# Moving chunk 1's logit transposes and maximum in the first gate/up, and building an edge constant with three GpSimd instructions

## The chip, the cores and the metric

The kernel runs on one core of a Trainium2 chip. A core has a matrix engine (TensorE, "PE" in the profile, its weight loads "PEld"), a vector engine (VectorE, "DVE"), an activation engine (ScalarE, "ACT"), a general engine (GpSimd, "POOL") and a queue engine that issues transfers (SyncE, "SP"). Each engine runs its own instruction stream in order and meets the others through semaphores. The metric is the device time of one execution in microseconds; of several executions the median counts.

## What is computed

One transformer block with modulation (adaLN). `x` is 2048 rows of 576 in bfloat16, `c` one row of 576. The two branches are an attention in which every row sees 8 earlier rows, two apart, and a gated feed-forward without a nonlinearity of width 4608. Cut to what matters:

```python
mod = (_silu(c) @ w_mod).reshape(c.shape[0], 6, 1, -1)
sa, ca, ga, sb, cb, gb = ...
h = _layernorm(x) * (1 + ca) + sa
x = x + ga * A(h)          # 32 heads of 18; idx = pos - 2 * arange(8), masked below 0
h = _layernorm(x) * (1 + cb) + sb
x = x + gb * (((h @ w_gate) * (h @ w_up)) @ w_down)
# A: logits = einsum('bhsd,bhswd->bhsw', q, k[idx]) / sqrt(18)
#    o = einsum('bhsw,bhswd->bhsd', softmax(logits), v[idx]);  o @ wo
```

## The kernel before

The 2048 rows are cut into 8 chunks of 256. A prologue (to about 48.7 us) computes the modulation and takes chunk 0 through its norm, its queries, keys and values and its attention. Then the chunks go through the feed-forward in the groups [0], [1, 2], [3, 4], [5, 6], [7]; for each group `gate_up` (L907) runs 36 row-tile pairs and `down` (L950) the product with `w_down`. A pair (`wg_pair`, L745) computes 128 columns of gate and of up: the contraction of 576 is four blocks of 128 rows and a rest of 64, and each matmul works on 64 rows, so that two of them share the PE array, one for `pg` (gate) and one for `pu` (up), each in a PSUM bank of its own. `first()` of a pair starts with the rest rows, whose weights lie in `wgr`, then takes the weights of its block (`wgu`, or `hh` for a block that was loaded there ahead of time); `second()` follows behind the next pair's `first()`. ACT copies `pu` (L796) and `pg` (L797) to SBUF, and in the first group DVE multiplies two pairs at a time into `hh` (L799).

Everything that the later chunks need before their turn runs between these pairs: in the first gate/up the attention of chunks 1 and 2, the norm of chunk 3 and its queries, keys and values, the norm of chunk 4, and the last part of the modulation. This work is cut into pieces, tuples of (PE time, DVE time, marks needed, mark set, delay of that mark, call). They are listed in threads, and a planner (`timed`, L847) sets them between the pairs with a simple clock of PE and DVE; in each step it takes the first thread whose next piece is ready. The order in which the calls are made is the order of the instructions on every engine; nothing is reordered afterwards.

The names that the change touches, with the lines of the kernel before:

- Chunk attention. `prod_t` (L485): products of q with the shifted k, one window position per instruction on DVE, eight per chunk. `b_l` (L494): PE sums them over the head dimension into `lgT`, four positions at a time; ACT copies `lgT` to `lgs` (L497). For chunk 1, `b_lt` (L505) has PE transpose `lgs` into a PSUM tile `lg`, four transposes; for the other chunks a transfer does it (L511, into `lg_t`). `b_sm0`: DVE takes the maximum `mx` over the eight positions (L521) and subtracts it into `dd` (L522). `b_exp` (L514): ACT's exponential of `dd`. Then `ssum` (L694), its reciprocal by ACT (L695, L697) and the shares `attn` (L702), the products with the shifted values `vsh` (L542) and their sums (L549 to L552) into `o_sb`. All PSUM tiles come from one pool of 8 banks: a bank that `lg` holds is free for a pair when `dd` has been written.
- Values. `v_sb` is stored to DRAM (`vd`, L470) and loaded back shifted (`vsh`, L479), both by POOL.
- Norm of a chunk: statistics on DVE (L281 to L285), ACT's roots and factors (L288 to L293), ACT's `xn` (L306), for chunk 3 in four pieces; a transposing transfer of `xn` into `hT` by SP (L418) and the modulation on DVE (L321).
- The last part of the modulation, `gb` (`gb_row` L1301, `gb_cols`): PE multiplies `sc_bc` with the last 576 columns of `w_mod` into `pa` (L378); ACT copies it (L381), and POOL stores it to DRAM (L382) and loads it back to all partitions (L383). The columns of `w_mod` are loaded by `load_wm5`: POOL clears a rest tile (L1055) and issues the load of 576 KB into a part of `hh` that is not in use yet (L1056) and of 72 KB into the rest tile, an `o_t` buffer (L1057). Right behind it POOL issues the first load of `w_down` (L174).
- Edge constant. In the prologue, chunk 0's second half of 128 rows takes shares of the first half's last rows through two constants, `edge` (L247 to L250) and `edge_t` (L252 to L256; 128 x 16 with ones at 2 + 18w + n for the seven positions w, n below 14 - 2w). PE reads `edge_t` in L608. `share_j` (L1139) makes chunk 0's shares on DVE (L1140), and `shift_attn` (L568) reads them on PE into `pz`.

Of the kernel before, what the change touches and what calls it, by code (L numbers as in the profile page):

```python
# [7 lines left out]
BF = mybir.dt.bfloat16  # L8
F32 = mybir.dt.float32
ALU = mybir.AluOpType  # L10
ACTF = mybir.ActivationFunctionType
AX = mybir.AxisListType
# [6 lines left out]
P = 128  # L19
# [6 lines left out]
W = 8  # L26
DIL = 2
FF = 4608
FT = FF // P
HALO = 16  # L30
SPAN = 14
# [14 lines left out]
def kernel(  # L46
# [13 lines left out]
    nc = tc.nc  # L60
# [31 lines left out]
    def ps(shape, dt, name):  # L92
        return psp.tile(shape, dt, name=name, tag="bank")

    def js(j):
        return slice(j * P, (j + 1) * P)
# [25 lines left out]
    def product(n):  # L122
        k0 = (prod_n[0] % (4 * CH // n)) * KT * n
        prod_n[0] += 1
        return prod_t[:, k0:k0 + KT * n].rearrange("p (k n) -> p k n", k=KT)

    sp_guard = tc.tile_pool(name="setup", bufs=1)
    sp = sp_guard.__enter__()
# [4 lines left out]
    def x_rows(i):  # L133
        return x_flat[i * CH:(i + 1) * CH, :].rearrange("(j p) d -> p j d", p=P)

    def load_x(i):
        if i < NCH:
            x_in[i] = xin.tile([P, ST, D], BF, name="x_t")
            nc.sync.dma_start(x_in[i][:], x_rows(i))
# [73 lines left out]
    for xn_t in xns:  # L213
# [12 lines left out]
                            pattern=[[-1, P + 2 * SPAN]], channel_multiplier=1)  # L226
# [4 lines left out]
    for k in range(2):  # L231
# [5 lines left out]
                            pattern=[[P, KT], [-DH, H]], channel_multiplier=1)  # L237
    nc.gpsimd.affine_select(out=ind[:], in_=ind[:], compare_op=ALU.is_ge, fill=0.0, base=DH - 1,
                            pattern=[[-P, KT], [DH, H]], channel_multiplier=-1)
    nc.gpsimd.memset(maskneg[:], 0.0)  # L240
    nc.gpsimd.affine_select(out=maskneg[:], in_=maskneg[:], compare_op=ALU.is_ge, fill=NEG,
                            base=-DIL * (W - 1), pattern=[[DIL, W], [0, H]], channel_multiplier=1)
    edge = sp.tile([P, W - 1, P], BF, name="edge")
    edge_t = sp.tile([P, 2 * HALO], BF, name="edge_t")[:, 0:HALO]
# [4 lines left out]
                            pattern=[[-(HALO + DIL), W - 1], [1, P]], channel_multiplier=-1)  # L249
    nc.gpsimd.affine_select(out=edge[0:HALO], in_=edge[0:HALO], compare_op=ALU.is_ge, fill=0.0, base=SPAN - 1,  # L250
                            pattern=[[-DIL, W - 1], [0, P]], channel_multiplier=-1)
    nc.gpsimd.memset(edge_t[:], 0.0)  # L252
    for w in range(W - 1):
        d = edge_t[:, 0:SPAN - DIL * w]
        nc.gpsimd.affine_select(out=d, in_=d, compare_op=ALU.not_equal, fill=1.0, base=-DIL - (HALO + DIL) * w,
                                pattern=[[-1, SPAN - DIL * w]], channel_multiplier=1)  # L256
    nc.gpsimd.memset(wo[64:, KF, :], 0.0)
    nc.gpsimd.memset(oT[64:, KF, :], 0.0)
    nc.gpsimd.memset(o_sb[:, :, D:], 0.0)
# [150 lines left out]
    def a_t(i, on_dve=True):  # L410
        a_tiles(i)
        hT = aa[i]["hT"]
        transposed(aa[i]["xn"], lambda m: hT[:, m, :], (0, 1), 0)(on_dve)
# [6 lines left out]
    def a_t4():  # L420
        a_t(4, False)
        nc.gpsimd.memset(aa[4]["hT"][64:, KF, :], 0.0)
# [27 lines left out]
    def a_q(i, g):  # L450
        qk_tiles(i, QGRP[g], slice(0, CH), nc.scalar.copy)
        if g == 2:
            a_halo(i)
# [34 lines left out]
    def b_l(i, w0):  # L488
        b = bb[i]
        prods = [b["prod"].pop(w0 + c) for c in range(4)]  # L490
        lgT = ps([P, CH], F32, "lgT")
        for m in range(KT):
            for c in range(4):
                nc.tensor.matmul(lgT[H * c:H * (c + 1), :], lhsT=ind[:, m, :], rhs=prods[c][:, m, :],  # L494
                                 start=(m == 0), stop=(m == KT - 1), skip_group_check=True)
        lgs = lgsp.tile([P, CH], BF, name="lgs")
        nc.scalar.copy(lgs[:], lgT[:])  # L497
        b.setdefault("lgs", []).append(lgs)

    def b_lt(i):  # L500
        b = bb[i]
        b["lg"] = ps([P, ST, W, H], BF, "lg")
        for w0, lgs in zip((0, 4), b.pop("lgs")):
            for j in range(ST):
                nc.tensor.transpose(b["lg"][:, j, w0:w0 + 4, :].rearrange("p w h -> p (w h)"), lgs[:, js(j)], ident[:])  # L505
# [7 lines left out]
    def b_exp(i):  # L513
        nc.scalar.activation(bb[i]["dd"][:], bb[i]["dd"][:], ACTF.Exp, scale=scale)  # L514
# [118 lines left out]
    def b_od(i):  # L633
        for j in range(ST):
            nc.sync.dma_start_transpose(out=oT[:, :, js(j)], in_=o_sb[:, j, :])
# [45 lines left out]
    def prods_of(i):  # L681
        r = []
        for w in (0, 4):
            r += [(0, 0.82, "", f"p{i}{v}", 1.0, lambda v=v: b_p(i, v)) for v in range(w, w + 4)]
            r += [(0.75, 0, f"p{i}{w + 3}", f"l{i}{w}", 1.0, lambda w=w: b_l(i, w)), (0, 0, f"l{i}{w}", f"t{i}{w}", 9.0 if i == 7 else 6.0, lambda w=w: b_ltd(i, w))]
        return r

    def softmax_of(i):
        b1 = lambda: b_sm1(i)
        if i in GROUPS[1]:  # L690
            def total():
                b = bb[i]
                ssum = small.tile([P, ST, H], F32, name="ssum")
                nc.vector.tensor_reduce(ssum[:], b["dd"][:].rearrange("p j w h -> p j h w"), axis=AX.X, op=ALU.add)  # L694
                nc.scalar.activation(ssum[:], ssum[:], ACTF.Ln)  # L695
                b["rs"] = small.tile([P, ST, H], F32, name="rs")
                nc.scalar.activation(b["rs"][:], ssum[:], ACTF.Exp, scale=-1.0)  # L697

            def shares():
                b = bb[i]  # L700
                b["attn"] = attnp.tile([P, ST, W, H], BF, name="attn")
                nc.vector.tensor_tensor(b["attn"][:], b.pop("dd")[:], b.pop("rs")[:, :, None, :].to_broadcast([P, ST, W, H]), ALU.mult)  # L702
            return [(0, 1.4, f"t{i}4", "y1", 0.0, lambda: b_sm0(i, False)) if i == 1 else (0, 1.4, f"t{i}4", f"s{i}", 1.1, lambda: b_sm0(i)), (0, 1.05, f"s{i}", f"r{i}", 0.9, total), (0, 0.72, f"r{i}", f"a{i}", 0.0, shares)]
        return [(0, 1.4, f"t{i}4", f"s{i}", 1.1, lambda: b_sm0(i)), (0, 2.4, f"s{i}", f"a{i}", 0.0, b1)]

    def values_of(i, nxt=None):
        r = []
        for j in range(ST):
            r += [(0, 0.75, f"a{i}", "-", 0, lambda j=j, w=w: b_mul(i, j, w)) for w in range(0, W, 2)]
            r += [(0, 0.75, "", "-", 0, lambda j=j: b_add(i, j, 0)), (0, 0.75, "", "-", 0, lambda j=j: b_add(i, j, 1)),  # L710
                  (0, 1.2, "", f"o{i}{j}", 0, lambda j=j: b_add(i, j, 2))]
            if nxt is not None:
                r.append((0, 0, f"v{nxt}", "-", 0, lambda j=j: b_ld(nxt, j)))
        return r

    def attention_of(c1, c2):
        p2, sm = prods_of(c2), softmax_of(c1)
        first = prods_of(c1) + p2[:4] + sm[:1] + p2[4:6] + sm[1:] + p2[6:]
        return first + values_of(c1, c2) + [(0, 0, "", "-", 0, lambda: b_od(c1))] + softmax_of(c2) + values_of(c2)
# [334 lines left out]
    def load_wm5():  # L1054
        nc.gpsimd.memset(wm5r[64:, :], 0.0)  # L1055
        nc.gpsimd.dma_start(wm5(), w_mod[0:KF * P, 5 * D:6 * D].rearrange("(k p) n -> p k n", p=P))  # L1056
        nc.gpsimd.dma_start(wm5r[0:64, :], w_mod[KF * P:D, 5 * D:6 * D])  # L1057
# [49 lines left out]
    def pj(j, w):  # L1107
        off = HALO - DIL * (W - 1 - w) + j * P
        prods[j, w] = product(P)
        nc.vector.tensor_tensor(prods[j, w], aa[0]["qT"][:, :, js(j)], aa[0]["kT"][:, :, off:off + P], ALU.mult)  # L1110
# [28 lines left out]
    def share_j(j):  # L1139
        nc.vector.tensor_tensor(attn0[:, j], dd0[:, j], sums.pop(j)[:, None, :].to_broadcast([P, W, H]), ALU.mult)  # L1140
# [50 lines left out]
        lj(1, w)  # L1191
    pj(1, 4)
    pj(1, 5)
    share_j(0)
    a_q(1, 1)
    shift_attn(0)
# [104 lines left out]
    def gb_row():  # L1301
# [2 lines left out]

    first = attention_of(1, 2)[12:-14]
    first = [(0, 0, "", "p17", 2.2, nop), (0.75, 0, "p17", "l14", 1.0, lambda: b_l(1, 4)), (0.35, 0, "l14", "t14", 0.3, lambda: b_lt(1))] + first
    second = attention_of(3, 4)
    second[1] = (*second[1][0:2], "n2", *second[1][3:])
    at = [k for k, p in enumerate(first) if p[2] == "v2"][0]
# [3 lines left out]
    first[at] = (0.6, 0, "o11", "-", 0, lambda: b_o(1))  # L1313
    gbg = {0: (qkv_of(3, "p17 z3"),
               [[(0, 0, "", "-", 0, lambda: (load_wm5(), load_wd(0))), (0, 0, "", "z3", 8.0, both_halves), (0, 0, "", "w5", 12.0, nop), (0.85, 0, "w5", "-", 0, gb_row), (0, 0, "", "-", 0, lambda: load_res(2))],
                first, [(0, 0, "y1", "s1", 0.6, lambda: b_exp(1))],
                norm_of(3, "", "", 5) + [(0, 2.5, "", "m4", 0.2, lambda: a_ln(4)), (0, 0, "m4", "r4", 1.0, lambda: aa[4]["rsq"]()),
                                         (0, 0, "r4", "e4", 2.0, lambda: aa[4]["norm"]((0,))), (0, 0, "e4", "n4", 1.6, lambda: aa[4]["norm"]((1,))),
                                         (0.6, 0, "n4 v3", "x4", 0, lambda: (a_t4(), load_x(6)))]]),
           1: (qkv_of(5, "p37"),  # L1320
               [[(0, 0, "", "-", 0, lambda: (loads_v(3), load_res(3), load_res(4)))], norm_of(5, "p33", "", 7), second]),
           2: (qkv_of(6, ""),
# [33 lines left out]
    for gi, grp in enumerate(GROUPS):  # L1356
        hh_t = hhp.tile([P, FT * 2 * CH], BF, name="hh")
        n = CH * len(grp)
# [45 lines left out]
```

## Time and profile before

| | before |
|---|---|
| median of 3 runs | 544.89 us (544.35 to 546.2) |
| profiled execution | 545.29 us |
| span of its profile | 543.6 us |
| mean granted TensorE clock | 1.000 |
| PE busy | 534.2 us (98%) |
| DVE busy | 316.4 us (58%) |
| ACT busy | 252.4 us (46%) |
| POOL busy | 71.1 us (13%) |

All times of the trace are microseconds from the span's start. A row of the timeline gives the start, the busy time, the engine, the line, the operation, what it writes and reads, the shape, and in square brackets the idle time of the engine before it with what ended that wait. Consecutive instructions of one kind are drawn together in one row with their count. A row that ends in "POOLq" or "PEldq" tells of an engine's queue: the semaphores that it went through ahead of an instruction. The line "DMA to landing" gives the time from a transfer's issue to its last byte's arrival, smallest, median and largest.

### The profile page before, as it was taken

The numbers are of one execution on the slowest core, as the hardware profiler recorded it, in microseconds if no ns is written. First come the engines' busy times: TensorE is split into PE (matmuls) and PEld (weight loads), VectorE is DVE, ScalarE is ACT, GpSimd is POOL, SyncE is SP. The second block draws the span as 40 slices with busy tenths as digits, with TensorE's granted clock in tenths as the row PEclk, the third lists the DMA queues.
The fourth block names the chain that finished last, engine by engine and source line by source line (L and its number), as shares of the span: only waits on it lengthen the run. The fifth ranks groups of instructions, "written<-read, shape, count | busy, mean of one in ns | idle before, by whom it ended". The sixth has DMA issues, their size and how long they took to land.

```text
span 543.6 us, 14637 instructions
## 1 busy us (share of the span) xinstructions
PE 534.2 (98%) x6196; PEld 319.4 (59%) x6196; DVE 316.4 (58%) x714; ACT 252.4 (46%) x625; POOL 71.1 (13%) x115
## 2 busy tenths in 40 slices
PE   7999899999999999999999999999999999999996
PEld 4887788756745444555544444555544445558874
DVE  4898687668776787636348896524344924032212
ACT  4866777544666553012646552013555551006630
POOL 8102104012000210111000110110010101110210
PEclk9999999999999999999999999999999999999999
DMA  9999999879862691978344982973397592859730
GB/s 280 295 286 339 335 265 326 310 128 322 264 196 86 223 316 45 235 208 299 119 119 151 247 272 65 211 237 112 95 240 216 151 315 68 244 145 297 260 89 26
DMA packets 94978, 114.67 MB, mean 211 GB/s; under 512 B 28001, under 2 KB 83698, under 8 KB 94786
## 3 DMA queue, kind: packets, MB, share of 16 engines
q1 hardware_dynamic: 83184, 67.14, 44.2%
q0 software_dynamic: 11424, 46.40, 27.5%
q8 instruction: 48, 0.79, 0.6%
q10 hardware_dynamic: 306, 0.21, 0.1%
q14 instruction: 16, 0.13, 0.1%
HBM read 103.29 MB, written 4.74 MB: 199 GB/s over the span
## 4 chain that ended last, share of the span: by engine, by line
PE 94%; DMA 3%; DVE 1%; ACT 1%; issue 1%; SPq 0%; ACTq 0%; DVEq 0%
PE pg L745 27%; PE pu L745 22%; PE acc L960 20%; PE pq L440 4%; PE pq L745 3%; PE pw L643 3%; PE accr L965 3%; PE acc L1015 3%; PE pv L745 2%; PE pv L463 2%; PE lgT L494 2%; DMA wmA<-in_w_mod_dram 1%; DMA lg_t<-lgs 1%; PE po L598 1%; PE pwj L620 0%
## 5 line engine op out<-in xcount | busy, mean ns | idle before, releaser
L745 PE MATMUL pg<-h2T,wgu 64*128 64x512 bf16 (+1 forms) x1376 | 266.2, 332 | 0.0
L745 PE MATMUL pu<-h2T,wgu 64*128 64x512 bf16 (+1 forms) x1376 | 264.3, 332 | 0.0
L745 PEld LDWEIGHTS <-wgu 64*128 64x128 bf16 x2752 | 134.8, 94 | 96.1 <-issue 1.1
L796 ACT CAST u_sb<-pu 128x512 bf16<-128x512 f32 (+1 forms) x172 | 85.6, 497 | 141.4 <-PE pg L745 138.6
L799 DVE TENSOR_TENSOR hh<-g_sb,u_sb 128x512 bf16<-128x512 bf16 x136 | 57.5, 423 | 114.2 <-ACT g_sb L797 113.6
L797 ACT CAST g_sb<-pg 128x512 bf16<-128x512 f32 (+1 forms) x172 | 86.9, 505 | 0.0
L960 PE MATMUL acc<-wd,hh 128*128 128x512 bf16 x344 | 86.1, 380 | 0.0
L960 PEld LDWEIGHTS <-hh 128*128 128x128 bf16 x504 | 48.9, 98 | 59.5 <-issue 1.3
L745 PE MATMUL pu<-h2T,wgr 64*128 64x512 bf16 (+1 forms) x188 | 61.6, 328 | 1.2 <-DVE dd L522 0.9
L965 PE MATMUL accr<-wd,hh 128*128 128x64 bf16 x344 | 62.4, 193 | 0.0
L745 PE MATMUL pg<-h2T,wgr 64*128 64x512 bf16 (+1 forms) x188 | 61.6, 327 | 0.0
L965 PEld LDWEIGHTS <-hh 128*128 128x128 bf16 x504 | 45.9, 98 | 1.9
L174 POOL DMA_DIRECT2D wd<-in_B_w_down_dram x29 | 21.8, 751 | 181.5 <-PE accr L965 100.1
L485 DVE TENSOR_TENSOR prod_t<-qT,kT 128x1280 bf16<-128x1280 bf16 x56 | 43.8, 818 | 1.7 <-PE lgT L494 1.0
L542 DVE TENSOR_TENSOR vsh<-vsh,attn 128x1152 bf16<-128x1152 bf16 x56 | 39.8, 751 | 0.0
L745 PEld LDWEIGHTS <-wgr 64*128 64x128 bf16 x376 | 18.8, 94 | 17.0 <-issue 3.2
L960 PE MATMUL acc<-prod_t,hh 128*128 128x512 bf16 x112 | 28.7, 380 | 0.0
L323 ACT ACTIVATE h2T<-h2T,modc 128x256 bf16<-128x256 bf16 x12 | 6.5, 592 | 40.9 <-DMA h2T<-xn 40.9
L479 POOL DMA_DIRECT2D vsh<-vd x14 | 12.5, 896 | 95.8 <-DVE o_sb L552 85.0
L440 PE MATMUL pq<-hT,wqk 128*128 128x256 bf16 (+1 forms) x225 | 21.7, 251 | 0.1
L745 PE MATMUL pq<-hT,wqk 64*128 64x256 bf16 (+1 forms) x360 | 21.7, 259 | 0.0
L965 PE MATMUL accr<-prod_t,hh 128*128 128x64 bf16 x112 | 21.6, 193 | 0.0
(212 smaller groups left out, 606.8 us busy)
## 6 DMA issues: line engine op xcount, KB each, us to landing
wgu<-in_B_w_gate_dram SPq DMA_DIRECT2D x41, 512.0 KB, 5.4
wgu<-in_B_w_up_dram SPq DMA_DIRECT2D x41, 512.0 KB, 7.3
wd<-in_B_w_down_dram POOLq DMA_DIRECT2D x29, 576.0 KB, 5.2
vsh<-vd POOLq DMA_DIRECT2D x14, 1152.0 KB, 9.4
prod_t<-in_B_w_down_dram POOLq DMA_DIRECT2D x8, 576.0 KB, 6.2
hh<-in_B_w_down_dram POOLq DMA_DIRECT2D x6, 576.0 KB, 6.8
x_t<-in_A_x_dram SPq DMA_DIRECT2D x8, 288.0 KB, 5.5
x_r<-in_A_x_dram SPq DMA_DIRECT2D x8, 288.0 KB, 9.4
```

The costliest lines, as they stand in the source:

```text
L174: return nc.gpsimd.dma_start(wb[:], B_w_down[r0:r0 + FB * P, :].rearrange("(k p) n -> p k n", p=P))
L440: nc.tensor.matmul(pq[:, gi, :], lhsT=wqk[:, kt, m * P:(m + 1) * P], rhs=hT[:, kt, cols], start=(kt == order[0] and not (by_k and gi)), st ...
L485: nc.vector.tensor_tensor(prod, aa[i]["qT"][:], aa[i]["kT"][:, :, off:off + CH], ALU.mult)
L542: nc.vector.tensor_tensor(v, v, at, ALU.mult)
L643: nc.tensor.matmul(pw[:], lhsT=oT[:, m, js(j)], rhs=wo[:, m, 0:512], start=(m == 0), stop=(m == KT - 1))
L745: return nc.tensor.matmul(out, lhsT=lhs, rhs=rhs, start=first, stop=last, skip_group_check=True)
L796: nc.scalar.copy(u[:, c, :], pu)
L797: nc.scalar.copy(g[:, c, :], pg)
L799: return lambda: nc.vector.tensor_tensor(hh[:, f - c:f + 1, :], g, u, ALU.mult)
L960: nc.tensor.matmul(acc[j][:], lhsT=hh[:, f, js(j)], rhs=wb[:, f % FB, 0:512], start=(f == 0), stop=(f == FT - 1))
L965: nc.tensor.matmul(accr[:, j, :], lhsT=hh[:, f, js(j)], rhs=wb[:, f % FB, 512:D], start=(f == 0 and j == 0), stop=(f == FT - 1), skip_grou ...
L1015: nc.tensor.matmul(acc[i][:], lhsT=hh[:, f, js(j)], rhs=wb(f)[:, c0:c1], start=(f == 0), stop=(f == FT - 1))
```

## The change

`edge_t` is no longer built by one memset and seven selects on POOL. Instead a new tile `edge_w` of 128 x 7 x 16 gets one memset and two selects that treat all seven window positions at once, and a DVE instruction in the prologue, between the last products of chunk 0's second half and `share_j(0)`, takes the maximum over the seven into `edge_t`.

In the first gate/up the list `first` (the attention of chunks 1 and 2) is put into another order at its head: indices 1 to 7 become 1, 3, 4, 2, 7, 5, 6. Index 1 is chunk 1's second logit product `b_l(1, 4)`, 2 its transposes `b_lt(1)`, 3 to 6 the first four products of chunk 2, and 7 `b_sm0` of chunk 1 (`mx` and `dd`). So the transposes come behind two products of chunk 2, `mx` and `dd` behind these, and the other two products last. The thread of chunk 3's and 4's norm moves ahead of `first` and of the thread that holds chunk 1's exponential, so the planner looks at it earlier in each step.

```diff
@@ -249,11 +249,12 @@
                             pattern=[[-(HALO + DIL), W - 1], [1, P]], channel_multiplier=-1)
     nc.gpsimd.affine_select(out=edge[0:HALO], in_=edge[0:HALO], compare_op=ALU.is_ge, fill=0.0, base=SPAN - 1,
                             pattern=[[-DIL, W - 1], [0, P]], channel_multiplier=-1)
-    nc.gpsimd.memset(edge_t[:], 0.0)
-    for w in range(W - 1):
-        d = edge_t[:, 0:SPAN - DIL * w]
-        nc.gpsimd.affine_select(out=d, in_=d, compare_op=ALU.not_equal, fill=1.0, base=-DIL - (HALO + DIL) * w,
-                                pattern=[[-1, SPAN - DIL * w]], channel_multiplier=1)
+    edge_w = sp.tile([P, W - 1, HALO], BF, name="edge_w")
+    nc.gpsimd.memset(edge_w[:], 0.0)
+    nc.gpsimd.affine_select(out=edge_w[:], in_=edge_w[:], compare_op=ALU.not_equal, fill=1.0, base=-DIL,
+                            pattern=[[-(HALO + DIL), W - 1], [-1, HALO]], channel_multiplier=1)
+    nc.gpsimd.affine_select(out=edge_w[:], in_=edge_w[:], compare_op=ALU.is_ge, fill=0.0, base=SPAN - 1,
+                            pattern=[[-DIL, W - 1], [-1, HALO]], channel_multiplier=0)
     nc.gpsimd.memset(wo[64:, KF, :], 0.0)
     nc.gpsimd.memset(oT[64:, KF, :], 0.0)
     nc.gpsimd.memset(o_sb[:, :, D:], 0.0)
@@ -1191,6 +1192,8 @@
         lj(1, w)
     pj(1, 4)
     pj(1, 5)
+    with nc.allow_low_precision("ones and zeros"):
+        nc.vector.tensor_reduce(edge_t[:], edge_w[:].rearrange("p w n -> p n w"), axis=AX.X, op=ALU.max)
     share_j(0)
     a_q(1, 1)
     shift_attn(0)
@@ -1304,6 +1307,8 @@
 
     first = attention_of(1, 2)[12:-14]
     first = [(0, 0, "", "p17", 2.2, nop), (0.75, 0, "p17", "l14", 1.0, lambda: b_l(1, 4)), (0.35, 0, "l14", "t14", 0.3, lambda: b_lt(1))] + first
+
+    first[1:8] = [first[1], first[3], first[4], first[2], first[7], first[5], first[6]]
     second = attention_of(3, 4)
     second[1] = (*second[1][0:2], "n2", *second[1][3:])
     at = [k for k, p in enumerate(first) if p[2] == "v2"][0]
@@ -1313,10 +1318,10 @@
     first[at] = (0.6, 0, "o11", "-", 0, lambda: b_o(1))
     gbg = {0: (qkv_of(3, "p17 z3"),
                [[(0, 0, "", "-", 0, lambda: (load_wm5(), load_wd(0))), (0, 0, "", "z3", 8.0, both_halves), (0, 0, "", "w5", 12.0, nop), (0.85, 0, "w5", "-", 0, gb_row), (0, 0, "", "-", 0, lambda: load_res(2))],
-                first, [(0, 0, "y1", "s1", 0.6, lambda: b_exp(1))],
                 norm_of(3, "", "", 5) + [(0, 2.5, "", "m4", 0.2, lambda: a_ln(4)), (0, 0, "m4", "r4", 1.0, lambda: aa[4]["rsq"]()),
                                          (0, 0, "r4", "e4", 2.0, lambda: aa[4]["norm"]((0,))), (0, 0, "e4", "n4", 1.6, lambda: aa[4]["norm"]((1,))),
-                                         (0.6, 0, "n4 v3", "x4", 0, lambda: (a_t4(), load_x(6)))]]),
+                                         (0.6, 0, "n4 v3", "x4", 0, lambda: (a_t4(), load_x(6)))],
+               first, [(0, 0, "y1", "s1", 0.6, lambda: b_exp(1))]]),
            1: (qkv_of(5, "p37"),
                [[(0, 0, "", "-", 0, lambda: (loads_v(3), load_res(3), load_res(4)))], norm_of(5, "p33", "", 7), second]),
            2: (qkv_of(6, ""),
```

## The prediction

> **What bounds the kernel now.** The first view is the page's table of busy times; the second lists what TensorE (PE) waited for over the whole span, in total, times and longest, in us.
>
> ```profile
> PE 534.2 (98%) x6196; PEld 319.4 (59%) x6196; DVE 316.4 (58%) x714; ACT 252.4 (46%) x625; POOL 71.1 (13%) x115
> PE pu L745 <- DVE dd L522: 0.9, 1, 0.9
> PE pa L378 <- ACT g_sb L797: 0.7, 1, 0.7
> ```
>
> PE is busy for 534.2 of 543.6 us, and the change takes no matmul away. So it can win only waits. These two lie at 61 to 64 us, in the first gate/up, where the change works; the four waits left out here stand in the prologue, before 49 us. Behind 64 us PE never waits again, so what is won reaches the end unless a new wait eats it. The third view is PE's timeline there.
>
> ```profile
> 57.35 0.27 PE L745 MATMUL pg<-h2T,wgr 64*128 64x256 bf16 x1
> 58.34 0.27 PE L745 MATMUL pg<-h2T,wgr 64*128 64x256 bf16 x1
> 59.35 0.27 PE L745 MATMUL pg<-h2T,wgr 64*128 64x256 bf16 x1
> 59.76 0.27 PE L745 MATMUL pu<-h2T,wgr 64*128 64x256 bf16 x1
> 60.65 0.27 PE L745 MATMUL pg<-h2T,wgr 64*128 64x256 bf16 x1
> 61.83 0.28 PE L745 MATMUL pu<-h2T,wgr 64*128 64x256 bf16 x1 [0.91 <-DVE dd L522]
> 63.69 0.43 PE L378 MATMUL pa<-hh,sc_bc 128*32 128x144 bf16 x16 [0.71 <-ACT g_sb L797]
> ```
>
> Each pg<-wgr row opens a pair of gate and up products; 57.35 to 58.34 is an undisturbed pair, 0.99 us. From 58.34 three pairs would bring PE to pa at 58.34 + 3 x 0.99 = 61.31; it gets there at 63.69. **2.38 us, or 0.44% of the time, is all that can be won.** It is lost in three places: before pu at 59.76, before pu at 61.83, before pa at 63.69.
>
> **The second loss is the one the change names.** Views: timelines of VectorE (DVE), ScalarE (ACT) and PE.
>
> ```profile
> 54.06 0.40 PE L505 MATMUL lg<-shifts,lgs 128*128 128x128 bf16 x4
> 56.84 0.38 ACT L797 CAST g_sb<-pg 128x256 bf16<-128x256 f32 x1
> 57.25 0.43 DVE L799 TENSOR_TENSOR hh<-g_sb,u_sb 128x512 bf16<-128x512 bf16 x1 [0.51 <-ACT g_sb L797]
> 57.59 1.55 DVE L485 TENSOR_TENSOR prod_t<-qT,kT 128x1280 bf16<-128x1280 bf16 x2
> 60.02 0.43 DVE L799 TENSOR_TENSOR hh<-g_sb,u_sb 128x512 bf16<-128x512 bf16 x1 [0.87 <-ACT g_sb L797]
> 60.36 0.68 DVE L521 TENSOR_REDUCE mx<-lg 128x64 f32<-128x512 bf16 x1
> 61.08 0.69 DVE L522 TENSOR_TENSOR dd<-lg,mx 128x512 f32<-128x512 bf16 x1
> ```
>
> Chunk 1's logits lg are transposed by 54.46, but mx and dd, which free their PSUM bank, stand in DVE's written order behind four products of chunk 2 and two hh. From the start of that hh to PE's pu is 61.83 - 60.02 = 1.81 us.
>
> **The change, part by part.** Chunk 3's norm, put ahead of the attention's pieces, takes no other work with it on PE, DVE or SyncE (SP); what moves is told here. **The four transposes** go two pairs later on PE; they cost the same 0.40 us, and the two pairs they let past are evicted about 0.33 us earlier (54.06 to the next pair at 54.40). So g_sb at 56.84 comes at 56.51 and ends at 56.89, and hh starts at 56.92; DVE is free for it: before its 57.25 it had idled for 0.51.
>
> **mx and dd** now follow this hh, ahead of the third and fourth product. By the same 1.81 us the bank is free at 56.92 + 1.81 = 58.73. In the new order the pair of 58.34 is the one that takes this bank, two pairs earlier than before. Its pu starts at 58.73 instead of some 0.1 behind its pg: a new wait of about 0.3 us. The pair then ends at about 59.62, and the next pu finds its bank, which ACT frees, at 59.76 as before: the first loss is swallowed by the new wait, not added to it. The pair after it starts at 60.65, as before, and its pu needs dd no longer: it runs through and PE is at pa at 60.65 + 0.99 = 61.64, 2.05 us sooner. The displaced products run from about 59.3, with the next hh between them at 60.02, to about 61.2; the logit product that reads them stands behind pa, later than that.
>
> **The exp** of chunk 1 (L514) moves forward on ACT, between chunk 3's xn and an eviction.
>
> ```profile
> 61.49 0.39 ACT L796 CAST u_sb<-pu 128x256 bf16<-128x256 f32 x1
> 62.92 0.37 ACT L796 CAST u_sb<-pu 128x256 bf16<-128x256 f32 x1 [0.42 <-PE pu L745]
> 65.11 0.63 ACT L514 ACTIVATE dd<-dd 128x512 f32<-128x512 f32 x1
> ```
>
> It puts 0.63 us ahead of the eviction of 61.49, which then ends with its g_sb at about 62.7, and the next, with an xn of 0.5 us between, at about 63.6. The pairs behind pa that want these banks come at about 63.7 and 64.7, so I take nothing; without that cover of 1 us it costs up to 0.63.
>
> **pa, the third loss**, is put down to ACT's g_sb, which was done long before. The true condition is in the rows of GpSimd (POOL) and of the loads; pa reads w_mod's last part, which POOL's L1056 loads into hh.
>
> ```profile
> 50.01 0.57 POOL L1055 MEMSET o_t<- 64x576 bf16 x1
> 56.79 0.76 POOL L1056 DMA_DIRECT2D hh<-in_w_mod_dram  x1 [6.21 <-DVE prod_t L485]
> L1056 POOLq EVENT_SEMAPHORE  x5: 17/43/43, 49.4 to 50.1; - x5
> DMA to landing us min/median/max: 6.8/6.8/6.8
> L378 PEldq EVENT_SEMAPHORE  x1: 51/51/51, 63.6 to 63.6; - x1
> ```
>
> Issued at 56.79, landed 6.8 later, 63.59; PE's weight queue passes its semaphore at 63.6 and pa starts at 63.69. **So if this load lands as before, the 2.05 us won ahead of pa are lost again in front of it**, all of them. Does the load move? Its five semaphores are passed by 50.1, the memset ahead of it ends at 50.58, and then POOL stands for 6.21 us with nothing that it waits for. The DMA table of 54 to 56 us shows what may have been missing:
>
> ```profile
> q0 software_dynamic: 152, 0.62, 90.9%
> q14 instruction: 1, 0.01, 1.5%
> ```
>
> One packet of program code came, from a queue that served none in the four us before. My reading, not shown by any row, is that it is POOL's, and that POOL stood for want of its next instructions. The edge constant speaks for a move: eight POOL instructions become three, and with their register moves eleven fewer stand ahead of L1056. A boundary in POOL's code that fell on L1056 then falls eleven instructions later, in a stretch where POOL waits anyway. L1056 would go out at about 50.6.
>
> When would it land? Behind it in time, queue q0 still holds the V loads (first row: one shift load, 10.3 us from its issue at 47.5; second row: V stores issued at 48.8 and 49.4); the three others are q0's packets, MB and share in 56 to 60, 57 to 59 and 59 to 61 us.
>
> ```profile
> DMA to landing us min/median/max: 10.3/10.3/10.3
> DMA to landing us min/median/max: 9.4/9.4/9.4
> q0 software_dynamic: 126, 0.44, 31.3%
> q0 software_dynamic: 33, 0.09, 12.3%
> q0 software_dynamic: 105, 0.44, 65.9%
> ```
>
> The last of these lands at 49.4 + 9.4 = 58.8, while q0 is nearly empty in 57 to 59 (0.09 MB): a gap that the early load fills. Its 576 and 72 KB are 0.66 MB: at 0.22 MB/us (59 to 61) it is moved by 57 + 3.0 = 60.0, plus the 1.8 us by which landing trails the empty queue, 61.8. Bounds: behind 58.8 without a gap but at the 0.31 MB/us of 54 to 56, 60.9; at the 0.11 of 56 to 60, 63.0 and 1.8, past 63.59, no gain. I take 61.8, nearest to the rows in which q0 had a load of this kind: pa at about 61.87, 1.82 us sooner.
>
> The Trainium skill speaks against my reading: "Runtime: NRT & Kernel Launch", section "Instruction fetch mechanics", says that an engine fetches its next page of code while it runs the current one and that a crossing is mostly hidden. By it the hole of 6.21 us isn't code, nothing moves it, and the sum ends at no change. The trace neither confirms nor refutes it, since the row doesn't name the packet's engine.
>
> **The edge constant** itself lies in the prologue. Views: timelines of POOL, DVE and PE.
>
> ```profile
> 10.52 1.76 POOL L255 TENSOR_SCALAR_AFFINE_SELECT edge_t<-edge_t 128x14 bf16<-128x14 bf16 x7
> 22.02 0.59 DVE L1134 TENSOR_REDUCE ssj<-dd 128x32 f32<-128x256 f32 x1
> 23.96 0.43 DVE L1140 TENSOR_TENSOR attn<-dd,ssj 128x256 bf16<-128x256 f32 x1 [0.54 <-ACT ssj L1136]
> 24.44 0.35 PE L568 MATMUL pz<-attn,shifts 128*128 128x32 bf16 x8
> ```
>
> Seven selects take 1.76 us; two of them, at most twice as long each for their wider rows, about 1.0, so POOL gains some 0.7 us; at four times the length each it would lose 0.2. Nobody waits for it there: PE's waits of the prologue name no POOL instruction. DVE gains one reduction, 112 elements a lane into 16; bounds 0 and the 0.59 of the 256-element one; I take 0.3. It stands just before attn at 23.96, in the 0.54 us that DVE idles for ACT: nothing. At 0.59 attn is 0.05 late, still ahead of pz.
>
> **Sum**, against the profiled execution's 545.29 (span 543.6): -2.38 + 0.33 (58.73 wait) + 0.23 (load) = -1.82, 543.47. The median of the runs is 544.89, 0.40 lower; there it gives **543.1**.
>
> **The rivals.** *A, the load lands as before* (the change doesn't reach the true condition): PE stands at pa from 61.64 to 63.6 instead of in two waits. For it: my reading of the hole rests on one packet, whose engine no row names. Against: no semaphore, and no other row, holds L1056. 544.9. By the section of the Trainium skill named above, this is the case to expect.
>
> *B, my forecast.* By its own bounds 542.8 (load before 61.64) to 543.9 (landing at 62.6).
>
> *C, POOL's hole moves on and bites later.* Eleven instructions on is a load at about 84 us; POOL's V shift for chunk 2 follows, and DVE's first use of it:
>
> ```profile
> 87.68 0.89 POOL L479 DMA_DIRECT2D vsh<-vd  x1 [1.97 <-DMA wgu<-in_B_w_up_dram]
> 101.06 1.43 DVE L542 TENSOR_TENSOR vsh<-vsh,attn 128x1152 bf16<-128x1152 bf16 x2
> ```
>
> A hole of 6.2 us there makes the shift about 4.2 late; at the 10.3 us of the earlier one it lands at 102.2 instead of 98.0, 1.1 behind its use, and TensorE's output projections, evicted behind it on DVE, wait up to as long: 543.1 + 1.1 = 544.2.
>
> *S, slower: the load lands later than before.* The hole stays, and PE, with its early pairs ahead, makes the weight request of 58.60 and chunk 3's transposes come sooner, before the load's packets.
>
> ```profile
> 58.60 0.37 SPq L157 DMA_DIRECT2D wgu<-in_B_w_gate_dram  x1
> DMA packets 1125, 1.44 MB, mean 360 GB/s; under 512 B 71, under 2 KB 1028, under 8 KB 1124
> ```
>
> All queues together move 0.36 MB/us there. Requests that come 0.33 us sooner put 0.12 MB ahead of it: +0.3, 545.2. If both halves of the weight request, 1.0 MB, go ahead, +2.9, 547.8. It decides from a landing later than 63.6, whatever DVE does; I take the middle, +1.6, 546.5. Against it: PE's pairs up to 58.34 are where they were, so the request hardly moves.
>
> **How the numbers follow.** B 0.48, A 0.18, C 0.10, S 0.24. About 0.3%, 1.6 us, can be told from no change here: faster is below 543.3, slower above 546.5. Of B 0.40 lies below 543.3 and 0.08 in between, where the load still gates pa by a part; A and C lie in between; of S, whose range is cut in the middle but which the whole request, x_r and the transposes behind it push upward, 0.16 lies above and 0.08 below. Faster 0.40, same 0.44, slower 0.16. The likeliest time is 543.1, B's own range 542.8 to 543.9. The range reaches from 542.5, B's end less 0.3 for what two runs differ by, to 546.4, which leaves out only S's upper part.
>
> **What would show it.** Right: mx and dd before 58.8; PE waits about 0.3 us for dd near 58.7 and nothing at 61; the load of L1056 issued near 50.6 and pa at 61.6 to 62.0; the reduction between two products of DVE, with pz of 24.44 unmoved. A: the same up to 61.6, and then some 2 us before pa with the load issued near 56.8. C: a hole on POOL near 84 us and a wait of PE for DVE after 101. S: a landing later than 63.6. The forecast is wrong if the load stays where it is, or if PE, 1.8 us ahead, meets behind 64 us a wait that has no row today.

## The result and the profile after

| | before | after |
|---|---|---|
| median of 9 runs each | 545.25 us (544.0 to 546.82) | 542.65 us (541.55 to 543.56) |
| ratio | | 0.9952 (95% interval 0.9937 to 0.9966) |
| span of the profile | 543.6 us | 541.7 us |

The changed kernel is faster by 2.6 us, 0.5% (1.9 to 3.4 us by the interval); 1.8 were forecast. The rows answer to those of before; behind the before's L256 the kernel after has line numbers larger by one, behind L1193 by three and behind L1306 by five (in e3, e4, e6 and e7 by three more). First PE's timeline, then DVE's and POOL's:

```profile
56.20 0.28 PE L746 MATMUL pg<-h2T,wgr 64*128 64x256 bf16 x1
58.18 0.27 PE L746 MATMUL pg<-h2T,wgr 64*128 64x256 bf16 x1
58.46 0.28 PE L746 MATMUL pu<-h2T,wgr 64*128 64x256 bf16 x1
59.34 0.27 PE L746 MATMUL pg<-h2T,wgr 64*128 64x256 bf16 x1
60.33 0.27 PE L746 MATMUL pg<-h2T,wgr 64*128 64x256 bf16 x1
60.43 0.27 PE L746 MATMUL pu<-h2T,wgr 64*128 64x256 bf16 x1
61.51 0.43 PE L379 MATMUL pa<-hh,sc_bc 128*32 128x144 bf16 x16
```

```profile
56.65 0.43 DVE L800 TENSOR_TENSOR hh<-g_sb,u_sb 128x512 bf16<-128x512 bf16 x1
56.99 0.68 DVE L522 TENSOR_REDUCE mx<-lg 128x64 f32<-128x512 bf16 x1
57.71 0.69 DVE L523 TENSOR_TENSOR dd<-lg,mx 128x512 f32<-128x512 bf16 x1
58.32 0.82 DVE L486 TENSOR_TENSOR prod_t<-qT,kT 128x1280 bf16<-128x1280 bf16 x1
```

```profile
50.28 0.57 POOL L1056 MEMSET o_t<- 64x576 bf16 x1
50.80 0.76 POOL L1057 DMA_DIRECT2D hh<-in_w_mod_dram  x1
51.55 0.55 POOL L1058 DMA_DIRECT2D o_t<-in_w_mod_dram  x1
DMA to landing us min/median/max: 9.1/9.1/9.1
```

mx and dd stand behind the hh of 56.65 and end before 58.5. Of the wait for dd some 0.2 us is left (58.18 to 58.46, where an undisturbed pg and pu lie 0.1 or less apart); the pairs of 59.34 and 60.33 run through. POOL goes from its memset to the load at once, and the load is there at 50.80 + 9.1 = 59.9, before PE comes. The margin varies: the same kernel profiled once more (e8) has the load issued at 50.62 and landed 10.6 us later, at 61.2, only 0.2 us before its pa.

The prologue does not take the same time in each execution (it waits for the first weights), so the stretch is measured from the first gate/up product. Before, this product starts at 48.71 and pa at 63.69: 14.98 us. The first row is of before, the second of after:

```profile
48.71 0.28 PE L745 MATMUL pg<-h2T,wgr 64*128 64x256 bf16 x1
48.56 0.28 PE L746 MATMUL pg<-h2T,wgr 64*128 64x256 bf16 x1
```

48.56 to 61.51, 12.95 us: **2.03 us less at pa**. A little is given back at once: right behind pa the last weight loads of lgT idle 0.27 us, and some 8 us later a pu idles 0.95, both on "issue", that is on no work or semaphore of the trace.

```profile
62.52 0.10 PEld L495 LDWEIGHTS <-ind 128*32 128x32 bf16 x3 [0.27 <-issue]
70.63 0.27 PE L746 MATMUL pu<-h2T,wgu 64*128 64x256 bf16 x1 [0.95 <-issue]
62.87 0.27 PE L746 MATMUL pg<-h2T,hh 64*128 64x256 bf16 x1
64.78 0.27 PE L745 MATMUL pg<-h2T,hh 64*128 64x256 bf16 x1
```

Up to the first product whose weights lie in hh, behind lgT (the third row; the last row is that of before), it is 14.31 us against 16.07, 1.76 less. From there to the end of the span it is 478.8 in both, after's 0.95 included; what these two waits are is taken up at the end.

### The profile page after: what moved, and what is told of

It is laid out like the page before. It is cut to its first block, busy times and chain, and to the rows that moved or that the text cites. A ratio compares the mean times of both kernels' runs of the same rounds, so it can differ in the third digit from the quotient of the medians.

```text
span 541.7 us, 14628 instructions
## 1 busy us (share of the span) xinstructions
PE 534.3 (99%) x6196; PEld 318.6 (59%) x6196; DVE 316.6 (58%) x715; ACT 252.5 (47%) x625; POOL 70.7 (13%) x110
## 4 chain that ended last, share of the span: by engine, by line
PE 97%; DMA 1%; DVE 0%; issue 0%; SPq 0%; ACT 0%
PE pg L746 29%; PE pu L746 23%; PE acc L961 20%; PE pq L441 4%; PE pq L746 3%; PE pw L644 3%; PE accr L966 3%; PE acc L1016 3%; PE lgT L495 2%; PE pv L746 2%; PE pv L464 2%; DMA wmA<-in_w_mod_dram 1%; PE po L599 1%; PE pwj L621 0%; PE accr L1019 0%; PE pwr L642 0%
```

## The experiments

Theory K: POOL stood ahead of the load for want of its code, and the smaller number of POOL instructions moved that place. Rival R: something else held the load, and the new order of the first gate/up freed it. In the table "stretch" is the time from the first gate/up product to the first one with weights from hh, which has the same work in all kernels, "load" the issue of w_mod's 576 KB, "wait" the longest of PE in the stretch; where PEld stands, it is of the weight loads, whose waits read some 0.2 to 0.3 us longer than PE's (1.18 and 0.91 for dd in before). Each run has one profile; the two of the kernel after (after, e8) differ by 0.19 us in the stretch.

| run | edge constant | first gate/up | idle memsets on POOL | load us | stretch us | wait us | ratio to before (95%) |
|---|---|---|---|---|---|---|---|
| before | old | old | 0 | 56.79 | 16.07 | dd 0.91 | |
| after | new | new | 0 | 50.80 | 14.31 | PEld 0.27 (issue) | 0.9952 (0.9937 to 0.9966) |
| e1 | new | old | 0 | 49.86 | 15.29 | dd 0.91 | 0.9974 (0.9958 to 0.9991) |
| e2 | old | new | 0 | 55.84 | 16.89 | load 2.71 | 1.0013 (0.9997 to 1.003) |
| e3 | new | new | 11 | 55.87 | 16.02 | load 1.89 | 1.0012 (0.9993 to 1.0031) |
| e4 | new | new | 9 | 50.04 | 14.44 | PEld 0.39 (issue) | 0.9967 (0.9952 to 0.9982) |
| e5 | new | list old, norm first | 0 | 50.11 | 14.67 | dd 0.16 (PEld 0.44) | 0.9957 (0.9937 to 0.9976) |
| e6 | new | new | 10 | 56.32 | 17.29 | load 2.38 | one execution, no ratio |
| e7 | new | new | 12 | 55.59 | 16.06 | load 1.95 | one execution, no ratio |
| e8 (after again) | new | new | 0 | 50.62 | 14.12 | hh 0.23 (PEld 0.51) | 0.9954 (0.9932 to 0.9976) |

### The edge constant alone (e1)

```diff
-    nc.gpsimd.memset(edge_t[:], 0.0)
-    for w in range(W - 1):
...
+    edge_w = sp.tile([P, W - 1, HALO], BF, name="edge_w")
...
+        nc.vector.tensor_reduce(edge_t[:], edge_w[:].rearrange("p w n -> p n w"), axis=AX.X, op=ALU.max)
     share_j(0)
```

> Before with only the new edge constant; the order of the first gate/up stays. Theory K (POOL's load of w_mod's last part was held by a boundary in POOL's code, which eleven fewer instructions move away): the load is issued at 50.5 to 51.0, PE still waits about 0.9 us for dd near 61.8, and pa starts at about 62.8 instead of 63.7; ratio to before 0.998. Rival R (the load is held by something that doesn't depend on the number of POOL instructions, and the new order of the first gate/up freed it): the load is issued at about 56.8, pa starts at 63.7, ratio 1.000.

Timelines of POOL and of PE in this run:

```profile
49.34 0.57 POOL L1056 MEMSET o_t<- 64x576 bf16 x1
49.86 0.76 POOL L1057 DMA_DIRECT2D hh<-in_w_mod_dram  x1
60.89 0.28 PE L746 MATMUL pu<-h2T,wgr 64*128 64x256 bf16 x1 [0.91 <-DVE dd L523]
61.97 0.43 PE L379 MATMUL pa<-hh,sc_bc 128*32 128x144 bf16 x16
```

K's forecast comes in. Nothing in the gate/up is reordered, dd keeps PE 0.91 us as before, yet the load goes out right behind the memset, and from this pu to pa it is 1.08 us instead of 1.86. That 0.78 is the whole difference of the stretches too (16.07 to 15.29), close to the 0.9 expected. The load was issued at 49.86 and not from 50.5 on, because this execution's first gate/up product, at 47.77, came 0.94 us earlier than that of before.

### The order alone (e2), and the count of POOL's instructions (e3, e4)

e2 is after with the old eight instructions for `edge_t` and without the DVE reduction. e3 and e4 are after with idle work on POOL in the prologue, eleven memsets in e3, nine in e4 (and ten in e6, twelve in e7):

```diff
     nc.gpsimd.memset(o_sb[:, :, D:], 0.0)
+    pad = sp.tile([P, HALO], BF, name="pad")
+    for _ in range(11):
+        nc.gpsimd.memset(pad[:], 0.0)
```

> After with the old edge constant, the order of the first gate/up as in after. K: the load is issued at about 56 to 57 again, the wait for dd is as short as in after (0.3), but PE stands some 2 us ahead of pa until about 63.5; ratio to before 0.999 to 1.001. R: load issued near 50.8, pa at 61.5, ratio 0.995 as after.

> After with eleven idle memsets of a 128x16 tile on POOL in the prologue, so that as many POOL instructions stand ahead of the load as before; the edge constant and the order are those of after. K: the hole is back in front of the load, issue at about 56 to 57, pa at about 63.5, ratio to before 0.999 to 1.001. R: as after, 0.995. If the old edge constant's own work mattered instead of its count, run e2 is slow and this one is not.

> The same with nine idle memsets. K: the boundary falls two instructions later than in the run with eleven, on the load of w_down that follows; w_mod's loads go out near 51, the w_down load only at about 57, where nobody needs it yet; pa at 61.5, ratio 0.995 as after. R, or a cost that grows with the number of instructions: not to be told from the run with eleven, with a ratio between 0.995 and 1.001 that hardly differs from it.

POOL's and PE's timelines of e2:

```profile
49.53 0.57 POOL L1055 MEMSET o_t<- 64x576 bf16 x1
55.84 0.76 POOL L1056 DMA_DIRECT2D hh<-in_w_mod_dram  x1 [5.73 <-PE lg L505]
63.55 0.43 PE L378 MATMUL pa<-hh,sc_bc 128*32 128x144 bf16 x16 [2.71 <-DMA hh<-in_w_mod_dram]
```

of e3 (eleven):

```profile
49.85 0.57 POOL L1059 MEMSET o_t<- 64x576 bf16 x1
55.87 0.76 POOL L1060 DMA_DIRECT2D hh<-in_w_mod_dram  x1 [5.45 <-DMA wqk<-in_A_wqkv_dram]
63.80 0.43 PE L382 MATMUL pa<-hh,sc_bc 128*32 128x144 bf16 x16 [1.89 <-DMA hh<-in_w_mod_dram]
```

and of e4 (nine):

```profile
49.52 0.57 POOL L1059 MEMSET o_t<- 64x576 bf16 x1
50.04 0.76 POOL L1060 DMA_DIRECT2D hh<-in_w_mod_dram  x1
50.79 0.56 POOL L1061 DMA_DIRECT2D o_t<-in_w_mod_dram  x1
51.33 0.80 POOL L174 DMA_DIRECT2D wd<-in_B_w_down_dram  x1
60.91 0.43 PE L382 MATMUL pa<-hh,sc_bc 128*32 128x144 bf16 x16
```

R falls. With the new order and the old edge constant the load is late again, and the wait for dd, down to some 0.2 us as in after, comes back as a wait for the load: PE stands 2.71 us before pa, named as such. So the order alone is worth nothing (1.0013). In e2 the load even landed 7.6 us behind its issue instead of 6.8, which makes its stretch 0.82 longer than before; e3 and e7 are as long as before, so this is not shown to be a price of the new order. e3 keeps the new edge constant and adds only instructions that do nothing: the hole of 5.45 us is back. Two of them fewer, and it is gone. It is the number of POOL instructions ahead of the load that decides, not what they do. Notice what the profile wrote behind the holes of before, e2 and e3: prod_t of DVE, lg of PE, wqk of a transfer. They are whatever ended shortly before; a releaser that changes from run to run while the hole stays is none.

Two expectations of e4 failed. With nine the hole was to fall on the load of w_down behind it, and that load went out at 51.33, at once. And the ratio was to be after's 0.995; it is 0.9967, with 0.995 just outside its interval, though pa starts 12.95 us behind the first gate/up product, as in after. e2 and e3 lie just above the 1.001 expected, within their intervals.

### One more and one fewer (e6, e7)

> After with ten idle memsets on POOL. If the boundary in POOL's code lies between the instructions that eleven and nine put there, the load of 576 KB goes out near 50 and the 72 KB behind it is held till about 56, with the last four matmuls of pa waiting to about 63; or all go out, as with nine, and one instruction is what decides.

> After with twelve idle memsets. By the code reading the hole is where it is with eleven or one instruction earlier, so the load is held till about 56 and PE waits some 2 us before pa. If the hole was a chance of the run with eleven, the load goes out near 50.

Ten and twelve hold the load as eleven does; of the two cases expected for ten neither came. e6:

```profile
56.32 0.76 POOL L1060 DMA_DIRECT2D hh<-in_w_mod_dram  x1 [6.00 <-PE lg L509]
57.07 0.56 POOL L1061 DMA_DIRECT2D o_t<-in_w_mod_dram  x1
63.43 0.58 PE L382 MATMUL pa<-hh,sc_bc 128*32 128x144 bf16 x16 [2.38 <-DMA hh<-in_w_mod_dram]
```

So one instruction, the tenth, decides over all three loads together. The traces bear the count out over all the kernels, whatever the instructions do. In the list of POOL's instructions the load of 576 KB is the 59th in after, e1, e5 and e8 and the 68th in e4, and it goes out at once; it is the 69th in e6, the 70th in before, e2 and e3 and the 71st in e7, and it is held. But the place isn't simply ahead of the 69th: e4's 69th and 70th, the two loads behind, were not held. A boundary that moves by one instruction for each one added would have held the 72 KB with ten, or the w_down load with nine. That it doesn't is not explained; where in POOL's stream the boundary lies stays open.

In e6's stretch not all is waiting. TensorE's granted clock was 0.50 in the window from 64 to 67 us, right behind the wait for the load, and from pa to the first weights in hh it took 1.89 us where e2, e3 and e7 took 1.09 to 1.16. Some 0.75 of the 17.29 us comes from this.

### The reordered list alone taken out (e5), and after once more (e8)

e5 is after without one line; the norm's thread stands first as in after.

```diff
-    first[1:8] = [first[1], first[3], first[4], first[2], first[7], first[5], first[6]]
```

> After without the reordered list of the first gate/up: edge constant and chunk 3's norm thread first as in after. If the norm's place moves nothing, as the prediction said, this is the run with the edge constant alone: PE waits 0.9 us for dd, some 1.1 us from pu to pa, ratio to before 0.997 to 0.998. If the norm's place does a share of the work, the wait for dd is shorter or PE's bank wait ahead of it is gone.

> After, once more. Its first profile has a PE wait of 0.95 us at 70.63 that ends on nothing the trace names, while a packet of PE's code that usually takes 1.1 us took 3.1. If that is a chance of one execution, it is smaller or gone here and the span is some 0.9 shorter; if the change makes it, it is here again. Ratio to before 0.994 to 0.996.

e5's timelines of PE (three rows) and of its weight loads (the last):

```profile
60.00 0.73 PE L495 MATMUL lgT<-prod_t,ind 128*32 128x256 bf16 x20
60.88 0.28 PE L746 MATMUL pg<-h2T,wgr 64*128 64x256 bf16 x1 [0.16 <-DVE dd L523]
61.97 0.43 PE L379 MATMUL pa<-hh,sc_bc 128*32 128x144 bf16 x16
60.88 0.10 PEld L746 LDWEIGHTS <-wgr 64*128 64x128 bf16 x2 [0.44 <-DVE dd L523]
```

The first case of the expectation failed, the second came. With the old list the norm's place does move PE work: lgT of chunk 2 now stands ahead of pa, not behind it, and fills 0.7 us of the time in which PE waited for dd. What remains of that wait is 0.16, of the 0.91 in e1 (0.44 of 1.19 in the weight loads). From e1 to e5 the stretch falls by 0.62, from e5 to after by 0.36 (to e8 by 0.55). So of the gain in the stretch the edge constant has 0.78, the norm's place some 0.6 and the list the rest; without the edge constant, e2 says, the last two are worth nothing. The ratios of e1, e5 and after have overlapping intervals and cannot rank the three; the stretches, of one profile each, can. The shares hold for this order of adding; the new list without the norm's place was not run.

e8's stretch to pa is that of after, 12.95, and it has no wait at 70.6, so that wait varies with the execution (e5 has one of 1.00, e1 and e4 none). But the span was expected 0.9 shorter without it, and it is 541.6, only 0.1 shorter: the wait cannot be read as 0.9 us of the time. Behind lgT its weights for the next pair idle 0.51 us, by the profile for a transfer into hh that was issued some 20 us earlier; what held them isn't settled.

```profile
63.08 0.11 PEld L746 LDWEIGHTS <-hh 64*128 64x128 bf16 x4 [0.51 <-DMA hh<-in_B_w_up_dram]
```

## Why the prediction was right

The likeliest case B came in, step by step.

- The bound of 2.38 us for all that can be won, and its three places: at pa after is 2.03 ahead.
- The remaining wait for dd: 0.3 forecast, about 0.2 measured; pu at 58.46 is 1.81 behind the hh of 56.65, the distance taken from before.
- The first loss: forecast as swallowed by the new wait, with the next pu still at 59.76. It is gone, and from 58.46 on no pair waits for a bank. ACT's eviction that ended just ahead of that pu starts 0.6 us earlier (0.45 against the first gate/up product); 0.33 was the forecast for the evictions. Before, then after:

```profile
59.35 0.36 ACT L796 CAST u_sb<-pu 128x256 bf16<-128x256 f32 x1
58.75 0.37 ACT L797 CAST u_sb<-pu 128x256 bf16<-128x256 f32 x1
```

- PE at pa: forecast 3.30 us after the opening pg of 58.34 without the load; 61.51 - 58.18 = 3.33. That it fits so well is partly luck: the three pairs were to take 1.28, 1.03 and 0.99 us and took 1.16, 0.99 and 1.18, the last with the step from a pair to pa, which the sum had left out.
- The load, the step on which the result hung: forecast to be issued near 50.6, issued at 50.80. Against rival A e1 and e3 show that the count of POOL's instructions moved it.
- Its landing is the term that was mis-sized: 61.8 forecast, 59.9 measured (61.2 in e8). The rate was too low. q0's packets in 54 to 56 us of the kernel after:

```profile
q0 software_dynamic: 174, 0.69, 95.9%
```

0.35 MB/us instead of the 0.22 that I took from 59 to 61 us of before, where the weights of SP shared the engines. The 0.23 us that the sum set for the load therefore fell away: 1.82 became 2.03.
- Not foreseen: the waits on "issue" behind pa. The first took 0.27 of it back at once. The second is a wait behind 64 us that has no PE row before, which the prediction had named as a sign of being wrong: it came, and with 0.95 us it was no small one. That the time behind the stretch was nevertheless 478.8 us in both, and that e8 lacks this wait, keeps the forecast standing.
- Wrong in itself, though without effect on the sum: that the norm's place takes no work with it. It holds between before and after, where the new list puts lgT back behind pa; e5 shows that alone it moves lgT.
- The exp cost nothing, as taken, but for another reason than the cover of 1 us: the eviction behind it was to move back by 0.63 and starts at 61.42, where before it was at 61.49, since ACT's xn ahead of the exp starts at 60.13 instead of 60.72. PE waits for no ACT.

```profile
60.90 0.65 ACT L515 ACTIVATE dd<-dd 128x512 f32<-128x512 f32 x1
61.42 0.39 ACT L797 CAST u_sb<-pu 128x256 bf16<-128x256 f32 x1
```

- The reduction took 0.35 us for the 0.3 forecast, and DVE still idled for ACT behind it; pz of PE follows 0.48 after attn, as before. That pz starts at 24.69 and not 24.44 is not its doing: the `ssj` reduction ahead of it is 0.26 later too.

```profile
23.59 0.35 DVE L1196 TENSOR_REDUCE edge_t<-edge_w 128x16 bf16<-128x112 bf16 x1
24.21 0.43 DVE L1141 TENSOR_TENSOR attn<-dd,ssj 128x256 bf16<-128x256 f32 x1 [0.27 <-ACT ssj L1137]
24.69 0.35 PE L569 MATMUL pz<-attn,shifts 128*128 128x32 bf16 x8
```

- Rival C did not come: at 84 us POOL has a gap of 0.19 us where 6.2 were feared.

```profile
83.43 0.75 POOL L174 DMA_DIRECT2D hh<-in_B_w_down_dram  x1 [0.19 <-issue]
```

The Trainium skill's page "Runtime: NRT & Kernel Launch", section "Instruction fetch mechanics", by which a crossing is mostly hidden, did not hold at this place, if the hole is one of code as its dependence on the count says: one instruction more or less on POOL made a hole of 5.5 to 6.2 us or none. At 84 us of the kernel after, its sentence fits.

The medians show 2.6 us where the stretch shows 1.8 to 2.0; the interval reaches down to 1.9. From the stretch's end to the span's end profiled executions of these kernels take 477.7 (e1) to 480.1 us (e3), so a difference of this size between two measurements needs no cause of its own. The record holds a possible one. A mean granted clock of 0.997 or less stands in 9 of 49 executions of before and in 11 of 24 of e2 and e3, and in none of the 48 of after, e1, e4, e5 and e8, where the load is early. In before, measured beside e8, such executions took 1.5 us longer (median 546.08 against 544.57), and without them e8 is 1.2 us below before instead of 2.2, while e2 and e3 stay within 0.2 us of before. Whether the late load brings the lower clock, as it looks in e6, no run shows.

## What to carry to other kernels

A change that removes one wait is worth nothing if the same engine soon waits for a second condition that ends as late as before: here the order without the load's move gave 1.0013, the load's move alone 0.9974, both together 0.9952. So look past the releaser that the profile names to the time at which each input was really there. And when an engine idles with all its semaphores passed, count the instructions ahead of it: a few more or fewer may move the hole.

## What the runs showed beside this

POOL is not the only engine that, after a wait without a named cause, goes on shortly behind a packet of program code. The trace's packets of program code, read from its list of packets (start, time taken, end, and when the engine went on):

```
queue 14 (POOL)       start   took   end     load issued   behind the end
before                54.76   0.49   55.25   56.79         1.54
e2                    53.91   0.37   54.28   55.84         1.56
e3 (eleven)           53.86   0.47   54.33   55.87         1.54
e6 (ten)              54.40   0.36   54.77   56.32         1.55
e7 (twelve)           53.56   0.49   54.04   55.59         1.55
queue 8 (PE)          start   took   end     PE goes on    behind the end
after                 59.85   1.14   60.99   62.52         1.53
e4                    59.42   1.18   60.60   62.05         1.45
before                69.04   1.08   70.12   71.59         1.47
e2                    69.06   1.06   70.12   71.65         1.53
after                 66.17   3.06   69.23   70.64         1.41
e5                    67.74   1.11   68.86   70.38         1.52
```

In all eleven the engine goes on 1.4 to 1.6 us behind the packet's end, in the five holes of POOL 1.54 to 1.56. after, e1, e5 and e8 have no packet of queue 14 between 50 and 78 us; e4 has one at 54.61 and no hole, as POOL had by then issued all that was due. That is what ties these packets to the holes; that queue 14's are POOL's, and queue 8's PE's, is inferred from it, since no row names the engine. By the same reading the "issue" waits of after's profile are PE waiting for its program:

```profile
70.64 0.09 PEld L746 LDWEIGHTS <-wgu 64*128 64x128 bf16 x1 [1.13 <-issue]
```

Here a packet of 16 KB took 3.06 us instead of 1.1. It varies with the execution: the weight loads wait 1.18 us at this place in e5, 0.17 in before and 0.30 in e2, and in the other six profiles not at all; the packet of e1 and e4 had ended by 67.2. POOL's packets came 3.4 to 4.2 us after POOL ran dry (50.58 to 54.76 in before), in a stretch where the transfer engines were busy throughout (share 1.01 to 1.14 in the windows from 50 to 56 us). In after the share in the same windows is 1.03 to 1.11, so busy queues go without a hole too. That they delay the code is argued from these times; no run changed those transfers by themselves.
